# Where two of the last tiles gather their outputs: the two PSUM banks of the scores in place of two of the six common ones

## The chip, the cores and the metric

The kernel runs on one core of a Trainium2 chip. Its time is the device time of that core in microseconds (us), lower is better. The engines are TensorE (PE in the profile, with its weight loads as PEld), VectorE (DVE), ScalarE (ACT), GpSimd (POOL) and SyncE (SP), which here only issues transfers. TensorE writes its results to PSUM, a memory of eight banks; one bank holds 512 float32 values on each of 128 partitions. VectorE and ScalarE read the results from there.

## The reference, cut to what matters

An attention whose keys and values are pooled 4x4 pixels of a feature map, and behind it a gated feed-forward block:

```python
kv_pool = kv.reshape(B, H // r, r, W // r, r, C).mean(axis=(2, 4))
k = v = kv_pool.reshape(B, -1, C) @ w_sr            # 768 keys of 128 for each of 4 batches
s = (q @ k.transpose(0, 2, 1)) / sqrt(C)
a = exp(s - s.max(-1)); a /= a.sum(-1)
x = a @ v                                           # 49152 rows of 128 in all
out = (maximum(x @ w_gate, 0) * (x @ w_val)) @ w_out  # 1536 hidden units
```

The division by the row's sum is done at the end: the block is of second degree in x, so that each output row is multiplied with the squared inverse of its sum.

## The kernel before, in words

The 49152 rows are cut into 96 tiles of 512 rows (`NT = 96`, `T = 512`), numbered 0 to 95. For each tile come the scores and their exponentials (`score_block`, `exp_block`), the turned exponentials (by a DMA), the weighted values x (`values`, `keep_values`), and then the feed-forward block in twelve pieces of 128 hidden units (`NFB = 12`). For piece n of a tile:

- "v": TensorE multiplies with w_val into one bank (`value_proj`, L504); "y": ScalarE copies that to SBUF as float16 (`keep_value`, L141).
- "g": TensorE multiplies with w_gate into another bank (`gate_proj`, L515); "h": VectorE takes the maximum with 0, multiplies it with the copied value and writes the piece of hT (`gated`, L523).
- "o": TensorE multiplies the piece with w_out and adds it in the bank of the tile's output (`out_proj`; L545, or four products of 128 columns by `out_add`, L529, in the last three tiles).

The PSUM is shared out in two ways. Six banks are common: `bank()` takes the one that has stood free longest from a list, and `freed()` puts a bank back at its end when the instruction that reads it is issued. The value and gate products, x and the outputs lie there. The other two banks are one tile, `wide_ps` of 128x1024 (a pool with a single buffer), which the scores of all tiles take in turn.

The order of the work on each engine is written out by hand. `STEADY` is the list of words for one round in the middle; in a round the scores of tile k, the x of tile k-2, the v, y, g and h of tile k-3 and the o of tile k-4 are interleaved. `DRAIN` is the list for the two rounds after the last scores, `LAST` the list of the round after these. In that last round TensorE goes through o, v, g for n from 0 to 11, with o of tile 94 and v and g of tile 95.

The last three tiles, 93 to 95, take their output in the order of rows. When all twelve pieces of tile 93 have been added, the word "oT" at the end of the second `DRAIN` round makes VectorE multiply the bank with the scale (`out_scale`, L587) and SyncE store it (`out_store`, L593). Tile 94 is scaled by ScalarE (L585) after the last round. Tile 95 is done by `out_last`: 48 products in three banks, three multiplications by VectorE, and the last store from ScalarE's queue.

So around the end the order on TensorE is: ..., g of the last piece of 94, o0 of 94, v0 and g0 of 95, o1 of 94, v1 and g1 of 95, and so on. On VectorE: ..., h of the last piece of 94, the scaling of tile 93, h0 to h11 of 95, the three multiplications of the last tile.

Of the kernel before, what the change touches and what calls it, by code (L numbers as in the profile page):

```python
# [9 lines left out]
FP32 = mybir.dt.float32  # L10
# [6 lines left out]
def kernel(  # L17
# [33 lines left out]
    T = 512  # L51
    NS = T // 128
    NST = N // T
    NT = B * NST
# [67 lines left out]
    def bank(shape, dtype=FP32):  # L122
        n = asked.pop() if asked else next(n for n in free_banks if n < usable[0])
        free_banks.remove(n)
        ps = pools[n // 6].tile(shape, dtype, tag=f"bank{n}", bufs=1, name="bank_ps")
        bank_numbers[id(ps)] = n, ps
        return ps
# [3 lines left out]
    def freed(ps):  # L131
        free_banks.append(bank_numbers.pop(id(ps))[0])
        return ps
# [238 lines left out]
    hTs, o_banks, o_left, o_sbs, vals = {}, {}, {}, {}, {}  # L372
# [155 lines left out]
    def out_add(k, fb, s, o_ps, first):  # L528
        nc.tensor.matmul(  # L529
            o_ps, hTs[k][:, fb, s * 128 : (s + 1) * 128], wo16[:, fb, :],  # L530
            start=first, stop=(fb == NFB - 1), skip_group_check=True,
        )

    def out_proj(k, fb):
        if k >= NT - 3:
            if fb == 0:
                o_banks[k] = bank([128, NS, 128])
            for s in range(NS):
                out_add(k, fb, s, o_banks[k][:, s, :], fb == 0 and s == 0)
            return  # L540
        first = k not in o_banks
        if first:
            o_banks[k], o_left[k] = bank([128, T]), NFB
        o_left[k] -= 1
        nc.tensor.matmul(  # L545
            o_banks[k], wo16[:, fb, :], hTs[k][:, fb, :], start=first, stop=o_left[k] == 0
        )
# [30 lines left out]
    def out_scale(k, engine, own, o_ps=None):  # L578
        if k not in o_sbs:
            o_sbs[k] = work.tile([128, NS, 128], FP32, tag="o_sb", bufs=3, name="o_sb")  # L580
        o_sb, o_ps = o_sbs[k][:, own], o_ps if o_ps is not None else freed(o_banks[k])
        scale = squares[k // 2][:, k % 2, own]
        if engine is nc.scalar:
            for s in range(o_sb.shape[1]):
                nc.scalar.mul(o_sb[:, s], o_ps[:, s], scale[:, s : s + 1])  # L585
        else:
            nc.vector.tensor_tensor(  # L587
                o_sb, o_ps, scale.rearrange("t (s o) -> t s o", o=1).to_broadcast(list(o_sb.shape)),
                op=ALU.mult,
            )  # L590
# [11 lines left out]
    def out_last(k):  # L602
        parts = [bank([128, 2, 128]), bank([128, 1, 128]), bank([128, 1, 128])]
        owns = [slice(0, 2), slice(2, 3), slice(3, 4)]
        o_banks[k] = None

        def add(s, fb0, fb1):
            n = max(s - 1, 0)
            for fb in range(fb0, fb1):
                out_add(k, fb, s, parts[n][:, s - owns[n].start], fb == 0 and s != 1)  # L610

        def keep(n, engine, queue=nc.sync):
            out_scale(k, engine, owns[n], parts[n])
            out_store(k, owns[n], queue)

        held = NFB - 2
        add(0, 0, held)
        add(1, 0, held)
        add(2, 0, held)
        add(0, held, NFB)  # L620
        add(1, held, NFB)
        keep(0, nc.vector)
        add(2, held, NFB)
        keep(1, nc.vector)
        add(3, 0, NFB)
        keep(2, nc.vector, nc.scalar)
# [51 lines left out]
    def open_step(word):  # L678
# [90 lines left out]
        elif head == "o":  # L769
            k, n = at[0], o_left.get(at[0], NFB)  # L770
            out_proj(*at)
            for queue in (nc.gpsimd, nc.sync):
                if out_moves:
                    queue.dma_start(*out_moves.pop())
            image_step(1, k, NFB - n)
        elif head == "oT":
            out_moves.extend(out_turn(at[0]))
        elif head == "k":
            q_turn_two(2, 0)
            q_load(3, range(2))  # L780
        elif head == "s":
            if not wides:
                opening.close()
                wides.append(
                    ctx.enter_context(
                        tc.tile_pool(name="psum_wide", bufs=1, space=bass.MemoryType.PSUM)
                    )
                )
            score_block(*at)
        elif head == "e":  # L790
            k, n = at
            exp_block(k, n)
            if n % 2:
                a_turn(k, n - 1, n + 1)
        else:
            raise ValueError(word)

    out_moves, moves, spread, wides = [], [], [], []
# [21 lines left out]
    for k in range(LEAD + 2, last + 1):  # L820
# [9 lines left out]
        for word in words:  # L830
            head, n = word.rstrip("0123456789"), int(word.lstrip("abcdefghijklmnopqrstuvwxyzADPT") or 0)
            if head == "o":
                out_proj(kO, n)
                if ph == 1 and n == NFB // 2:
                    q_load(g + 2, [1])
# [7 lines left out]
            elif head == "oT":  # L843
                if kO < NT - 3:
                    out_moves.extend(out_turn(kO))
                elif k < last:
                    out_scale(kO, nc.vector, slice(0, NS))
                    out_store(kO, slice(0, NS))
# [12 lines left out]
            elif head in ("tb", "P", "pk"):  # L861
                pair, since = divmod(at - 6 if head == "tb" else at - 8, 4)
# [7 lines left out]
            elif LEAD <= kV < NT:  # L870
                if head == "x":
                    values(kV, n)
                else:
                    keep_values(kV)
    out_scale(last - LAG - 1, nc.scalar, slice(0, NS))
    out_store(last - LAG - 1, slice(0, NS))
    out_last(last - LAG)
# [30 lines left out]
```

## Time and profile before

| | us |
|---|---|
| median of 3 runs | 1024.41 (1024.4 to 1024.45) |
| the profiled execution, its own time | 1024.25 |
| its span, first to last instruction | 1022.5 |
| TensorE busy | 1017.2 (99%) |
| ScalarE busy | 918.5 (90%) |
| VectorE busy | 869.4 (85%) |
| GpSimd busy | 524.0 (51%) |

Times in the trace count from the start of the span. A row of the timeline gives the start, the length, the engine, the line, the operation with what it writes and reads, and how many equal instructions stand together. A TensorE row's length (0.38 us for a product of 512 columns) reaches over the start of the next, since products are pipelined; what TensorE needs for one is the distance from start to start. Line numbers are those of the kernel before.

### The profile page before, as it was taken

The page shows a single profiled execution, that of the slowest core. Times are in us where ns is not written, and L with a number is a line of the kernel's source. Part 1 is how long each engine was busy: PE and PEld are TensorE (multiplying, and loading weights), DVE is VectorE, ACT ScalarE, POOL GpSimd, SP SyncE. Part 2 cuts the span into 40 slices and gives each one's busy share as a digit, 9 for nine tenths or more (in the row PEclk, how much of TensorE's full clock was granted, in tenths as well). Part 3 has the DMA queues.
Part 4 walks back from the last instruction along what each step waited for, and adds up shares of the span by engine and source line. Part 5 has one row for each costly group of instructions (what it writes and reads, how often), then busy time and mean ns, then how long its engine had stood idle before and what let it go on. Part 6 is the DMA issues. An engine that isn't in the chain of part 4 may idle for free.

```text
span 1022.5 us, 17480 instructions
## 1 busy us (share of the span) xinstructions
PE 1017.2 (99%) x5021; PEld 485.2 (47%) x5021; DVE 869.4 (85%) x1450; ACT 918.5 (90%) x1927; POOL 524.0 (51%) x1312
## 2 busy tenths in 40 slices
PE   9999999999999999999999999999999999999998
PEld 4444444444444444444444444444444444444445
DVE  5988888888888888888888888888888888888888
ACT  5999998999999999999999999999999999999986
POOL 3487857344437576544434856754434543443342
PEclk9999999999999999999999999999999999999999
DMA  9999999878799999868779999978787878777651
GB/s 317 172 171 184 186 211 145 140 122 132 132 198 156 201 164 184 136 116 143 125 134 201 165 186 187 157 131 137 128 130 114 147 122 129 124 119 124 98 91 44
DMA packets 475743, 153.48 MB, mean 150 GB/s; under 512 B 451584, under 2 KB 465920, under 8 KB 475648
## 3 DMA queue, kind: packets, MB, share of 16 engines
q1 hardware_dynamic: 453184, 126.08, 65.9%
q0 software_dynamic: 22032, 25.19, 17.6%
q10 hardware_dynamic: 432, 1.11, 0.3%
q8 instruction: 39, 0.64, 0.3%
q14 instruction: 56, 0.46, 0.2%
HBM read 53.94 MB, written 26.35 MB: 79 GB/s over the span
## 4 chain that ended last, share of the span: by engine, by line
PE 99%; DMA 1%; DVE 0%; ACTq 0%; issue 0%
PE bank_ps L504 24%; PE bank_ps L515 24%; PE bank_ps L545 24%; PE wide_ps L397 12%; PE bank_ps L439 12%; PE bank_ps L529 1%; DMA kv_in<-in_kv_dram 1%; PE bank_ps L456 1%; PE bank_ps L378 1%; PE wide_ps L336 0%; PE bank_ps L300 0%; PE bank_ps L314 0%; PE bank_ps L474 0%; DVE kv_s L272 0%; PE bank_ps L209 0%; ACTq L246 0%
## 5 line engine op out<-in xcount | busy, mean ns | idle before, releaser
L523 DVE SCALAR_TENSOR_TENSOR hT<-bank_ps,val 128x512 f16<-128x512 f32 x1152 | 727.3, 679 | 104.4 <-PE bank_ps L515 83.7
L141 ACT CAST val<-bank_ps 128x512 f16<-128x512 f32 x1149 | 628.4, 596 | 44.4 <-PE bank_ps L504 23.9
L504 PE MATMUL bank_ps<-xT,wv 128*128 128x512 f16 x1152 | 421.0, 379 | 0.0
L515 PE MATMUL bank_ps<-xT,wg 128*128 128x512 f16 x1152 | 376.3, 379 | 0.0
L545 PE MATMUL bank_ps<-hT,wo 128*128 128x512 f16 x1116 | 348.7, 379 | 0.0
L402 ACT ACTIVATE a<-wide_ps 128x768 f16<-128x768 f32 x368 | 302.2, 821 | 44.0 <-PE wide_ps L397 44.0
L397 PE MATMUL wide_ps<-kv,qT 128*128 128x512 f16 x736 | 179.8, 326 | 0.0
L439 PE MATMUL bank_ps<-aT,kv 128*128 128x512 f16 x552 | 179.0, 379 | 0.0
L558 POOL TENSOR_TENSOR o_sb<-o_t,scale 128x512 f32<-128x512 f32 x89 | 93.2, 1047 | 158.8 <-issue 141.0
L545 PEld LDWEIGHTS <-wo 128*128 128x128 f16 x1116 | 109.1, 98 | 132.1 <-issue 0.5
L515 PEld LDWEIGHTS <-wg 128*128 128x128 f16 x1152 | 112.6, 98 | 122.5 <-issue 0.2
L504 PEld LDWEIGHTS <-wv 128*128 128x128 f16 x1152 | 112.5, 98 | 105.4 <-issue 0.4
L423 POOL COPY scale<-square 32x8 f32<-32x8 f32 x736 | 141.2, 192 | 28.6
L416 POOL TENSOR_TENSOR square<-inverse 128x8 f32<-128x8 f32 x46 | 9.3, 202 | 248.9 <-DVE inverse L414 248.9
L838 POOL DMA_DIRECT2D out_dram<-o_sb x208 | 130.3, 632 | 9.6 <-POOL o_sb L558 7.4
L397 PEld LDWEIGHTS <-qT 128*128 128x128 f16 x736 | 71.9, 98 | 87.0 <-issue 0.2
L447 DVE CAST xT<-bank_ps 128x512 f16<-128x512 f32 x92 | 63.6, 691 | 31.7 <-PE bank_ps L439 31.6
L439 PEld LDWEIGHTS <-kv 128*128 128x128 f16 x552 | 53.9, 98 | 65.2
L402 ACT ACTIVATION_READ_ACCUMULATOR a<-wide_ps 128x1 f32 x368 | 76.1, 207 | 0.0
L553 DVE STREAM_TRANSPOSE o_t<-bank_ps 128x512 f32<-128x512 f32 x93 | 65.4, 703 | 0.3 <-PE bank_ps L504 0.2
L162 POOL DMA_DIRECT2D q<-in_q_dram x84 | 48.8, 581 | 0.3 <-issue 0.3
L256 POOL TENSOR_TENSOR s<-kv_in 128x512 f32<-128x512 f32 x36 | 45.1, 1281 | 0.7
(86 smaller groups left out, 210.8 us busy)
## 6 DMA issues: line engine op xcount, KB each, us to landing
kv_in<-in_kv_dram SPq DMA_DIRECT2D x42, 512.0 KB, 5.3
out_dram<-o_sb SPq DMA_DIRECT2D x177, 64.0 KB, 3.6
q<-in_q_dram POOLq DMA_DIRECT2D x88, 128.0 KB, 3.4
out_dram<-o_sb POOLq DMA_DIRECT2D x176, 64.0 KB, 4.2
aT<-a SPq DMA_TRANSPOSE x184, 4.5
kv_line<-in_kv_dram SPq DMA_DIRECT2D x4, 512.0 KB, 9.8
placed<-blocks SPq DMA_DIRECT2D x9, 128.0 KB, 2.5
kvT<-placed SPq DMA_DIRECT2D x36, 32.0 KB, 2.2
```

What stands on the lines that cost most here:

```text
L141: nc.scalar.copy(to, what)
L397: nc.tensor.matmul(s_ps[:, j0 * 128 : j1 * 128], qT, kv16[:, b, j0:j1, 0:C], start=True, stop=True)
L402: nc.scalar.activation(a16s[k][:, s, :], s_banks.pop(s)[:, 0:J], AF.Exp, scale=qk_scale, accum_out=a_sums[k // 2][:, k % 2, s : s + 1],)
L423: nc.gpsimd.tensor_copy(to[32 * b : 32 * (b + 1), :, :, j], squares[k // 2][32 * j : 32 * (j + 1)])
L439: nc.tensor.matmul(x_banks[k], kv16[:, k // NST, jc, C : 2 * C], aT[:, jc], start=first, stop=x_left[k] == 0,)
L504: nc.tensor.matmul(proj_banks["v", k, fb], wv16[:, fb * 128 : (fb + 1) * 128], xTs[k], start=True, stop=True,)
L515: nc.tensor.matmul(proj_banks["g", k, fb], wg16[:, fb * 128 : (fb + 1) * 128], xTs[k], start=True, stop=True,)
L523: nc.vector.scalar_tensor_tensor(hTs[k][:, fb, :], freed(proj_banks.pop(("g", k, fb))), 0.0, vals.pop((k, fb)), op0=ALU.max, op1=ALU.mult,)
L545: nc.tensor.matmul(o_banks[k], wo16[:, fb, :], hTs[k][:, fb, :], start=first, stop=o_left[k] == 0)
L553: nc.vector.transpose(o_t, freed(o_banks.pop(k)))
L558: nc.gpsimd.tensor_tensor(to, o_by, scale.to_broadcast([128, NS, 4, 32]), op=ALU.mult)
L838: queue.dma_start(*out_moves.pop())
```

## The change

The gathering bank of tiles 93 and 94 is no longer taken by `bank()` at each tile's first piece. At the first piece of tile 93 one `wide_ps` tile is taken from the pool of the scores, and its two halves of 512 columns, a bank each, become the gathering places of tiles 93 and 94. The scores of all tiles are done by then. `out_scale` no longer gives a bank back, since none was taken from the list. Nothing else is edited; the lists of words and the number of instructions stay as they are.

```diff
     def out_proj(k, fb):
         if k >= NT - 3:
-            if fb == 0:
-                o_banks[k] = bank([128, NS, 128])
+            if k == NT - 3 and fb == 0:
+                pair = wides[0].tile([128, 1024], FP32, tag="wide", name="wide_ps")
+                for i in range(2):
+                    o_banks[k + i] = pair[:, i * T : (i + 1) * T].rearrange(
+                        "t (s c) -> t s c", s=NS
+                    )
             for s in range(NS):
                 out_add(k, fb, s, o_banks[k][:, s, :], fb == 0 and s == 0)
             return
@@
-        o_sb, o_ps = o_sbs[k][:, own], o_ps if o_ps is not None else freed(o_banks[k])
+        o_sb, o_ps = o_sbs[k][:, own], o_ps if o_ps is not None else o_banks[k]
```

## The prediction

> **What bounds the kernel now.** I read the page's engine shares and its chain first, then the stretches around the change, then the timelines of the three engines there. The page says that the chain which ended last is TensorE almost alone.
>
> ```profile
> PE 1017.2 (99%) x5021; PEld 485.2 (47%) x5021; DVE 869.4 (85%) x1450; ACT 918.5 (90%) x1927; POOL 524.0 (51%) x1312
> ...
> PE 99%; DMA 1%; DVE 0%; ACTq 0%; issue 0%
> ```
>
> The change touches nothing ahead of the first output product of tile 93, the first of these in TensorE's timeline, so only the last 20 us are in question.
>
> ```profile
> 1002.14 0.61 PE L529 MATMUL bank_ps<-wo,hT 128*128 128x128 f16 x8
> ```
>
> The stretches there (PE, PEld, DVE, ACT and POOL busy, then the granted clock):
>
> ```profile
> 1000.00:1005.00 5.00, 5.00 (x43) 2.99 (x42) 4.97 (x9) 3.99 (x9) 3.70 (x6) 1.00 0.16 26
> 1005.00:1010.00 5.00, 5.00 (x52) 3.26 (x49) 4.74 (x9) 3.06 (x6) 1.74 (x4) 1.00 0.19 30
> 1010.00:1015.00 5.00, 5.00 (x45) 3.14 (x45) 5.00 (x8) 4.25 (x8) 0.00 (x0) 1.00 0.14 52
> ```
>
> TensorE and VectorE are both full here, and the granted clock is 1.00. Whether TensorE waits at all is seen from start to start:
>
> ```profile
> 1008.06 0.38 PE L515 MATMUL bank_ps<-xT,wg 128*128 128x512 f16 x1
> 1008.27 0.39 PE L529 MATMUL bank_ps<-wo,hT 128*128 128x128 f16 x4
> 1008.50 0.38 PE L504 MATMUL bank_ps<-xT,wv 128*128 128x512 f16 x1
> 1008.71 0.38 PE L515 MATMUL bank_ps<-xT,wg 128*128 128x512 f16 x1
> 1008.93 0.39 PE L529 MATMUL bank_ps<-wo,hT 128*128 128x128 f16 x4
> 1009.15 0.38 PE L504 MATMUL bank_ps<-xT,wv 128*128 128x512 f16 x1
> 1009.45 0.38 PE L515 MATMUL bank_ps<-xT,wg 128*128 128x512 f16 x1
> 1009.66 0.39 PE L529 MATMUL bank_ps<-wo,hT 128*128 128x128 f16 x4
> 1010.05 0.39 PE L504 MATMUL bank_ps<-xT,wv 128*128 128x512 f16 x1
> 1010.27 0.38 PE L515 MATMUL bank_ps<-xT,wg 128*128 128x512 f16 x1
> ...
> 1015.95 0.38 PE L504 MATMUL bank_ps<-xT,wv 128*128 128x512 f16 x1
> 1016.17 0.38 PE L515 MATMUL bank_ps<-xT,wg 128*128 128x512 f16 x1
> 1016.42 2.84 PE L529 MATMUL bank_ps<-wo,hT 128*128 128x128 f16 x48
> ```
>
> 1008.06 is the gate product of tile 94's last piece, 1008.27 is o0 of tile 94, 1008.50 and 1008.71 are v0 and g0 of tile 95, and so on; 1010.05 is v2, 1016.17 is g11, and the 48 products are the last tile's. Unhindered, a product starts 0.21 to 0.23 after the one before, and a group of o, v, g takes 0.66 (1008.93 - 1008.27). Between 1008.27 and 1010.05 lie seven steps, three o at 0.225 and four v or g at 0.215, which is 1.535; 1.78 passed. So TensorE loses 0.25 here to waits for banks (0.09 at g1, 0.17 at v2), and after v2 almost nothing: (1016.17 - 1010.27) / 9 = 0.656 a group. All that this stage could give back is that 0.25, and some 0.03 ahead of the 48 products. VectorE and ScalarE:
>
> ```profile
> 1005.48 3.92 DVE L523 SCALAR_TENSOR_TENSOR hT<-bank_ps,val 128x512 f16<-128x512 f32 x6 [0.19 <-ACT val L141]
> 1009.31 0.68 DVE L587 TENSOR_TENSOR o_sb<-bank_ps,square 128x512 f32<-128x512 f32 x1
> 1009.91 7.77 DVE L523 SCALAR_TENSOR_TENSOR hT<-bank_ps,val 128x512 f16<-128x512 f32 x12
> ```
> ```profile
> 1008.91 1.24 ACT L141 CAST val<-bank_ps 128x512 f16<-128x512 f32 x2 [1.12 <-PE bank_ps L504]
> 1010.48 6.48 ACT L141 CAST val<-bank_ps 128x512 f16<-128x512 f32 x10 [0.32 <-PE bank_ps L504]
> ```
> ```profile
> PEld L504 <- DVE o_sb L587: 0.2, 1, 0.2
> ```
>
> VectorE runs six h pieces of tile 94 without a gap, 0.65 each, and scales tile 93 right behind them: that ends at 1009.31 + 0.68 = 1009.99, 1.72 after o0 of tile 94 was begun. v2 at 1010.05 is the product that got tile 93's bank: it started 0.06 after the scaling ended, which the wait above names.
>
> **The change part by part.** *The first half.* o0 of tile 93 used to wait for a copy by ScalarE that freed its bank; now it takes the scores' banks, whose last reader finished over a round ago. Cost nothing, gain nothing: that product started without a gap before.
>
> *One more common bank.* While tile 93 gathers, and again while tile 94 does, v and g turn over six banks, not five. The most this can give is the 0.28 above, least nothing; the next part takes it all.
>
> *The second half, and a new wait.* Tiles 93 and 94 now share one tile, `wide_ps`. The tile framework keeps order tile by tile, and in the program as built o0 of tile 94, the first product into the second half, waits for VectorE's scaling of tile 93, the last reader of the first half. Before, o0 had a bank of its own and waited only for an h piece four instructions earlier on VectorE. No row shows the new wait itself; its ends are known. TensorE reaches o0 at 1008.27; the scaling ends at 1009.99. I take 0.06 for the hand-over, as at v2, so that o0 starts at 1010.05: a stall of 1.78. It cannot be shorter by much, since VectorE has no gap from 1005.48 on and its inputs came from a TensorE that was not held up until then; the 0.19 gap before, which waited for a ScalarE copy, is the most that could come off it. The ends are thus 1.59 and, with the 0.2 of the waits row as the hand-over, 1.92.
>
> *What is queued behind it.* Products start in order, so v0, g0 and all that follows of tile 95 come later, as do ScalarE's copies and VectorE's h0 to h11. After o0 come the same steps: v2 starts at 1010.05 + 1.535 = 1011.585, not at 1010.05, which is +1.535; the 0.25 of waits before is in that difference, since it falls away.
>
> *Whether the rest catches up or falls further behind.* TensorE can't catch up: from v2 on it goes at 0.656 a group before and after, and before only the 0.03 at 1016.42 can be won. Does VectorE hold it up? A copy starts 0.41 after its v (1008.91 - 1008.50) and, from the last, ends 1.01 after it (1010.48 + 6.48 - 1015.95); h11 ends 1.73 after v11 (1009.91 + 7.77 - 1015.95). With six banks v of piece n+3 takes the bank of v of piece n: free after 1.01, wanted after 1.97. g of piece n+3 takes that of g: free after 1.73, wanted after 2.19. That leaves 0.4 after the hand-over, and h at 0.65 keeps pace with groups of 0.656. VectorE's head start is gone (its queue idles from 1009.99 until h0 at about 1011.4), but nothing waits for it. In the last tile, the first product that needs h10 comes after g11's step of 0.22 and 30 of the 48 products, 30 x 2.84 / 48 = 1.78: 2.2 after v11, while even h11 is ready after 1.73. So the 48 products start about 1.5 later and run as before, and the last multiplications and stores follow them as before. Tile 93's store is issued at the same time as before, since its scaling is; ScalarE's scaling of tile 94 and its store move with tile 94, and end ahead of the last tile's as they did. No instruction or transfer is added on any queue.
>
> The sum: +1.535 less 0.03, say **+1.5 us**. Against the profiled execution's 1024.25 that is 1025.75; its 1024.25 lies 0.16 under the median of the runs, 1024.41, so that I put the changed kernel at **1025.9**, 0.15% slower. A difference of under 0.2% (2.05 us, up to 1026.46) is counted as no change here.
>
> **A rule beside the row.** The Trainium skill's page "PSUM — Partial Sum Buffer", section "PSUM bank collisions raise a hardware error", says that accesses are to be guarded by bank and quadrant. The two halves are different banks, so by that rule the chip asks for no wait here, and o0 would start at 1008.27; the sum would be the gain of at most 0.28, or 1024.1. No run here shows two engines in the two halves at once, and the wait that the program holds decides, so the sum goes by that.
>
> **The rivals.**
> *No wait between the halves.* The two halves hold different data, and nothing in the computation orders them. Then only the sixth bank counts: 1024.41 - 0.28 to 1024.41, say 1024.2. Against it stands the wait in the built program.
> *Slower than 0.2%: the granted clock falls in the pause.* TensorE's longest pause in these 20 us is now 0.17; the new one is ten times that. If the clock were halved after it, a group would take 1.31 in place of 0.66. From 0.55 us of loss on (1026.46 - 1025.9), so 1.1 us at half clock, the change counts as slower. Ends: no time at half clock, 1025.9; all that is left, twelve groups of 0.656 and 2.84, which is 10.7 us more. If it lasts as long as the pause, it is 0.9 more: 1026.8. No row of before has a granted clock under 1.00, so nothing in it speaks for this. The Trainium skill, "TensorE: Matmul & The Clock Gate", part 1, gives the half clock to an idle window of about 3.4 us; by that rule a pause of 1.78 is too short, and the time stays 1025.9.
> *VectorE becomes the bound of the last round.* It now starts h0 without a backlog and has 0.4 of slack per piece; a hand-over 0.05 slower on each of twelve pieces would eat it and add 0.2 to 0.6: 1026.1 to 1026.5. Against it: the 12 pieces of before already run at 0.65 each.
>
> **How the numbers follow.** The new wait with its price of 1.5: 0.74. VectorE as the bound: 0.09, a third of it beyond 1026.46. The clock: 0.12, nearly all beyond. No wait between the halves: 0.03. Something that I don't see: 0.02, on either side. So slower by over 0.2%: 0.16; within 0.2%: 0.83; faster: 0.01, since 0.28 is all there is to win. The range goes from 1025.3 (the stall shortened by 0.19, a profile that stands 0.16 closer to the runs and some 0.2 for the readings) to 1026.7 (a hand-over of 0.2, VectorE's 0.6).
>
> **What would show it.** In TensorE's timeline a gap of about 1.8 ahead of the first four L529 products of tile 94, at 1008.3 to 1010.05, put down to VectorE's scaling; VectorE idle for some 1.4 after it and h pieces that then follow v by 1.7; no gap at g1 and v2; the 48 products at about 1017.95; a span of about 1024.0; the granted clock at 1.00. I am wrong if o0 starts at 1008.3 (no wait), if the groups after it take over 0.66 (the clock or VectorE), or if the scaling itself comes at another time.

## The result, and the profile after

The changed kernel takes 1025.84 us in the median of 22 runs (1025.63 to 1026.69), the kernel before 1024.40 in 22 (1024.2 to 1024.82). The ratio is 1.0015, with a 95% interval of 1.0009 to 1.0021: 1.44 us slower, where 1.5 was forecast.

The profiled execution of the changed kernel took 1026.69, 0.85 over its median. The waits of TensorE over its whole span say where that came from. A row names who waited, for whom, and for how long in total, how often, and the longest:

```profile
PE wide_ps L529 <- DVE o_sb L591: 1.6, 1, 1.6
...
PE bank_ps L439 <- DMA aT<-a: 0.8, 1, 0.8
```

The second row is a late transfer of turned exponentials, work that the change doesn't touch; TensorE has no such wait in the profile of before. It leaves everything behind it 0.95 us later than before (the gate product of tile 94's last piece starts at 1009.01, there at 1008.06), so places are compared from that product on. The first row is the new wait. TensorE's timeline around it (line 529 keeps its number, 587 has become 591):

```profile
1009.01 0.38 PE L515 MATMUL bank_ps<-xT,wg 128*128 128x512 f16 x1
1011.00 0.38 PE L529 MATMUL wide_ps<-wo,hT 128*128 128x128 f16 x4 [1.61 <-DVE o_sb L591]
1011.22 0.38 PE L504 MATMUL bank_ps<-xT,wv 128*128 128x512 f16 x1
1011.43 0.38 PE L515 MATMUL bank_ps<-xT,wg 128*128 128x512 f16 x1
1011.65 0.39 PE L529 MATMUL wide_ps<-wo,hT 128*128 128x128 f16 x4
1011.87 0.38 PE L504 MATMUL bank_ps<-xT,wv 128*128 128x512 f16 x1
1012.09 0.38 PE L515 MATMUL bank_ps<-xT,wg 128*128 128x512 f16 x1
1012.31 0.39 PE L529 MATMUL wide_ps<-wo,hT 128*128 128x128 f16 x4
1012.53 0.38 PE L504 MATMUL bank_ps<-xT,wv 128*128 128x512 f16 x1
1012.75 0.38 PE L515 MATMUL bank_ps<-xT,wg 128*128 128x512 f16 x1
...
1018.64 0.38 PE L515 MATMUL bank_ps<-xT,wg 128*128 128x512 f16 x1
1018.86 2.84 PE L529 MATMUL bank_ps<-wo,hT 128*128 128x128 f16 x48
```

o0 of tile 94 starts 1.99 after the gate product, not 0.21: a stall of 1.78 from start to start. The trace counts 1.61, since it lets the gate product's 0.38 run out first; below, "pause" is this shorter figure. From o0 to the 48 products there is no other gap. VectorE and ScalarE in the same stretch:

```profile
1006.43 3.92 DVE L523 SCALAR_TENSOR_TENSOR hT<-bank_ps,val 128x512 f16<-128x512 f32 x6 [0.19 <-ACT val L141]
1010.26 0.68 DVE L591 TENSOR_TENSOR o_sb<-wide_ps,square 128x512 f32<-128x512 f32 x1
1012.25 7.90 DVE L523 SCALAR_TENSOR_TENSOR hT<-bank_ps,val 128x512 f16<-128x512 f32 x12 [1.31 <-PE bank_ps L504]
```
```profile
1011.63 7.79 ACT L141 CAST val<-bank_ps 128x512 f16<-128x512 f32 x12 [2.89 <-PE bank_ps L504]
```

The scaling of tile 93 ends at 1010.94, and o0 follows 0.06 later. VectorE, which went on to h0 at once before, now idles 1.31 for it.

### The profile page after: what moved, and what is told of

It reads as the page before. It is cut to its first block, busy times and chain, and to the rows that moved or that the text cites. A ratio compares the mean times of both kernels' runs of the same rounds, so it can differ in the third digit from the quotient of the medians.

```text
span 1024.9 us, 17486 instructions
## 1 busy us (share of the span) xinstructions
PE 1017.0 (99%) x5021; PEld 485.4 (47%) x5021; DVE 869.9 (85%) x1450; ACT 919.5 (90%) x1927; POOL 524.7 (51%) x1312
## 4 chain that ended last, share of the span: by engine, by line
PE 97%; DMA 2%; DVE 0%; issue 0%; ACTq 0%; DVEq 0%
PE bank_ps L504 24%; PE bank_ps L515 24%; PE bank_ps L549 23%; PE wide_ps L397 12%; PE bank_ps L439 12%; DMA aT<-a 1%; DMA kv_in<-in_kv_dram 1%; PE bank_ps L456 1%; PE bank_ps L378 1%; PE wide_ps L529 0%; PE wide_ps L336 0%; PE bank_ps L300 0%; PE bank_ps L529 0%; PE bank_ps L314 0%; DVE hT L523 0%; PE bank_ps L474 0%
```

## The experiments

All times are medians; those of before are from runs on the same chip, beside each. The runs with three and with one and a half scalings were on another chip than the others. The theory is that the loss is one wait, of the first product into the second half for the reader of the first half, and that it is there only because both halves have one name. The rival is that the place costs: these banks, or the clock.

**The same banks under two names.** The pool of `wide_ps` is closed ahead of tile 93 and a pool of two one-bank tiles opened in its place.

```diff
-                pair = wides[0].tile([128, 1024], FP32, tag="wide", name="wide_ps")
+                scores_psum.close()
+                tail = ctx.enter_context(tc.tile_pool(name="psum_tail", bufs=1, space=PSUM))
                 for i in range(2):
-                    o_banks[k + i] = pair[:, i * T : (i + 1) * T].rearrange(...)
+                    o_banks[k + i] = tail.tile([128, NS, 128], FP32, tag=f"tail{i}", name="tail_ps")
```

> The changed kernel, but the two banks of the scores are handed over as two tiles of one bank each, one for tile 93 and one for tile 94; the banks, the order of the work and the instructions stay. Theory (the wait is one between the two halves, there only because they have one name): o0 of tile 94 no longer waits for VectorE's scaling of tile 93, the stall of 1.78 us is gone, and the sixth common bank gives back up to 0.28: 1024.1 to 1024.4. Rival (the place costs, whatever it is called: these banks, or the clock after them): 1025.8 as in the changed kernel.

Measured: 1024.03 (1023.83 to 1024.39, 11 runs), beside 1024.37 for before; ratio 0.9997 (0.9988 to 1.0006). The timeline of TensorE, from the same gate product:

```profile
1008.48 0.38 PE L516 MATMUL bank_ps<-xT,wg 128*128 128x512 f16 x1
1008.70 0.39 PE L530 MATMUL tail_ps<-wo,hT 128*128 128x128 f16 x4
...
1010.01 0.39 PE L530 MATMUL tail_ps<-wo,hT 128*128 128x128 f16 x4
...
1016.34 0.38 PE L516 MATMUL bank_ps<-xT,wg 128*128 128x512 f16 x1
1016.56 2.84 PE L530 MATMUL bank_ps<-wo,hT 128*128 128x128 f16 x48
```
```profile
1009.73 0.68 DVE L593 TENSOR_TENSOR o_sb<-tail_ps,square 128x512 f32<-128x512 f32 x1
```

o0 starts 0.22 after the gate product, and from the gate product to the 48 products pass 8.08 us, in the kernel before 8.36: the pause is gone, and so are the 0.28 of waits for want of a sixth bank. While VectorE scales tile 93 out of one of the two banks (1009.73 to 1010.41), TensorE adds o2 of tile 94 in the other, from 1010.01 on. The stall came from the shared name, not from the place. That this version is faster than the kernel before is seen in the trace; the medians say the same, but the ratio's interval doesn't leave 1.

**Half of the change: only tile 93 in the scores' banks.**

```diff
-                for i in range(2):
-                    o_banks[k + i] = pair[:, i * T : (i + 1) * T].rearrange(...)
+                o_banks[k] = pair[:, 0:T].rearrange("t (s c) -> t s c", s=NS)
+            elif fb == 0:
+                o_banks[k] = bank([128, NS, 128])
```

> Half of the change: tile 93 gathers in the scores' banks, tile 94 in a common bank. Theory: no stall at o0 of tile 94; five banks for v and g in the last round as before, so v3 waits about 0.2 us for h0: 1024.3 to 1024.4. Rival (the place costs): half of the loss at least, 1025.1 or more.

Measured: 1024.31 beside 1024.37, ratio 1.0002 (0.9994 to 1.0011). No stall at o0; v3 is the late product, with 0.41 from the start before it where 0.22 is the rule. VectorE begins h0 at 1010.01 and needs some 0.69 for it, which agrees with the forecast that v3 waits for it:

```profile
1010.34 0.39 PE L529 MATMUL bank_ps<-wo,hT 128*128 128x128 f16 x4
1010.75 0.38 PE L504 MATMUL bank_ps<-xT,wv 128*128 128x512 f16 x1
```

**The other half: only tile 94 there**, in the second bank, with tile 93's common bank given back after its scaling.

```diff
-            if k == NT - 3 and fb == 0:
+            if k == NT - 2 and fb == 0:
                 pair = wides[0].tile([128, 1024], FP32, tag="wide", name="wide_ps")
-                for i in range(2):
-                    o_banks[k + i] = pair[:, i * T : (i + 1) * T].rearrange(...)
+                o_banks[k] = pair[:, T : 2 * T].rearrange("t (s c) -> t s c", s=NS)
+            elif fb == 0:
+                o_banks[k] = bank([128, NS, 128])
...
-                    out_scale(kO, nc.vector, slice(0, NS))
+                    out_scale(kO, nc.vector, slice(0, NS), freed(o_banks[kO]))
```

> The other half: tile 93 gathers in a common bank, which comes back after its scaling, tile 94 in the second bank of the scores. Theory: no reader of the first half, so no stall at o0; g2 is the product that gets tile 93's bank, wanted at about the time when the scaling ends: 1024.1 to 1024.4. Rival (the place costs): 1025.1 or more.

Measured: 1024.14 beside 1024.37, ratio 0.9999 (0.999 to 1.0008). o0 starts 0.21 after the gate product. Either half alone costs nothing that can be measured; only the two together do.

**The wait kept, but covered.** The o of tile 94 stands three pieces later in the last round.

```diff
-    LAST = [f"{head}{n}" for n in range(NFB) for head in "ovygh"] + ["oT"]
+    LAST = [
+        word for n in range(NFB + 3)
+        for word in [f"o{n - 3}"] * (n >= 3) + [f"{head}{n}" for head in "vygh"] * (n < NFB)
+    ] + ["oT"]
```

> The changed kernel, with the o of tile 94 put three pieces later in the last round's list: v0, g0, v1, g1, v2, g2 of tile 95 come first, then o0. Theory: the wait stays, but 1.29 us of products cover it; 0.49 of it is left, and g3 waits some 0.16 for h0: 0.65 in place of 1.78, about 1024.7, between 1024.4 and 1025.0. Rival (the place or the clock costs): 1025.8.

Measured: 1024.82 beside 1024.37, ratio 1.0006 (0.9997 to 1.0015).

```profile
1009.18 0.38 PE L507 MATMUL bank_ps<-xT,wv 128*128 128x512 f16 x1
1009.49 0.38 PE L518 MATMUL bank_ps<-xT,wg 128*128 128x512 f16 x1
1010.09 0.38 PE L532 MATMUL wide_ps<-wo,hT 128*128 128x128 f16 x4 [0.22 <-DVE o_sb L594]
1010.31 0.38 PE L507 MATMUL bank_ps<-xT,wv 128*128 128x512 f16 x1
1010.69 0.38 PE L518 MATMUL bank_ps<-xT,wg 128*128 128x512 f16 x1
```

Against steps of 0.215, g2 is 0.09 late, o0 0.38 and g3 0.16: 0.63 in all, where 0.65 was expected (0.49 at o0, of which g2 has already taken 0.09, and 0.16 at g3). The same wait for the same scaling costs a third as much when TensorE has other products to run first.

**The reader on another engine.** ScalarE scales tile 93.

```diff
-                    out_scale(kO, nc.vector, slice(0, NS))
+                    out_scale(kO, nc.scalar, slice(0, NS))
```

> The changed kernel, with tile 93 scaled by ScalarE, which idles there, in place of VectorE: four instructions of 1.14 us together, free to start at about 1008.3 by the times of before, when the last o product of tile 93 is in its bank, not behind two h pieces. Theory: o0 of tile 94 starts at about 1009.5 in place of 1010.05, the stall is some 1.2: about 1025.3. Rival (the stall has to do with VectorE's read of a PSUM bank or with the clock, not with the last reader of the first half): no stall, 1024.1 to 1024.4, or 1025.8.

Measured: 1025.26 beside 1024.40, ratio 1.0009 (1.0 to 1.0018). The pause follows the reader, whichever engine it is on:

```profile
1008.24 0.38 PE L515 MATMUL bank_ps<-xT,wg 128*128 128x512 f16 x1
1009.68 0.38 PE L529 MATMUL wide_ps<-wo,hT 128*128 128x128 f16 x4 [1.06 <-ACT o_sb L589]
```
```profile
1008.49 1.14 ACT L589 ACTIVATE o_sb<-wide_ps,square 128x128 f32<-128x128 f32 x4 [0.52 <-PE wide_ps L529]
```

ScalarE ends at 1009.63 and o0 starts 0.05 later; the stall is 1009.68 - 1008.24 - 0.21 = 1.23.

**The wait made longer.** The scaling issued twice.

```diff
                     out_scale(kO, nc.vector, slice(0, NS))
+                    out_scale(kO, nc.vector, slice(0, NS))
```

> The changed kernel, with VectorE's scaling of tile 93 issued twice, one right behind the other (the second writes the same values again). Theory: o0 of tile 94 waits for the second, which ends 0.60 to 0.68 later (1009.31 to 1009.91 is start to start, 0.68 one length): the stall grows to about 2.4 and the time to 1026.4 to 1026.5. Rival (the stall is of a fixed length, or VectorE's queue has room): 1025.8.

Measured: 1027.03, seven runs from 1026.39 to 1028.21, beside 1024.40; ratio 1.0029 (1.0018 to 1.004). The profiled execution, 1026.56, shows a longer pause and nothing else. From start to start the stall is 2.50, where about 2.4 was expected; the pause is 2.33, 0.72 over the changed kernel's 1.61:

```profile
PE wide_ps L529 <- DVE o_sb L591: 2.3, 1, 2.3
```

But the median is above the forecast of 1026.4 to 1026.5, and the runs lie in two groups. So it was run again, and beside it the two tiles of the first experiment with the scaling issued twice.

> The shared tile with two scalings once more, since its seven runs lay between 1026.39 and 1028.21. Theory: the stall is 0.65 to 0.72 longer than with one scaling, as its trace shows, and what goes beyond 1026.5 is scatter that comes from elsewhere: a median of 1026.4 to 1026.6. Rival: a median of 1027 again, so that the second scaling costs about twice its length.

> The two banks handed over as two tiles, and tile 93 scaled twice by VectorE. Theory: o0 of tile 94 still doesn't wait; the second scaling moves h0 0.65 later, and g3, which gets g0's bank when h0 has read it and was ready 0.09 before that with one scaling, now waits some 0.6: about 1024.6, 0.6 over the two tiles with one scaling and 1.8 or more under the shared tile with two. Rival (two scalings cost by themselves more than their 0.65, as the median of the shared tile with two, 1.2 over that with one, may say): 1025.2 or more.

Measured: 1028.20 for the shared tile (seven runs, 1026.56 to 1028.42), ratio 1.0031 (1.002 to 1.0042): the forecast of 1026.4 to 1026.6 failed. The two tiles with two scalings took 1024.75 (1024.59 to 1024.82, 11 runs) beside 1024.32, ratio 1.0004 (0.9995 to 1.0013), where about 1024.6 was forecast; there, a second scaling costs about its length (0.72) and no more. The second profile of the shared tile is of an execution of 1028.42, and shows the rest. Stretches (busy times of PE, PEld, DVE, ACT and POOL, then the granted clock):

```profile
1005.00:1010.00 5.00, 3.73 (x42) 2.51 (x39) 4.76 (x8) 2.34 (x5) 2.02 (x4) 1.00 0.21 34
1010.00:1012.00 2.00, 0.94 (x9) 0.64 (x9) 0.98 (x2) 0.30 (x1) 0.00 (x0) 0.91 0.06 22
1012.00:1014.00 2.00, 2.00 (x12) 1.17 (x11) 1.21 (x2) 0.87 (x2) 0.00 (x0) 0.50 0.29 110
1014.00:1016.00 2.00, 2.00 (x14) 1.15 (x13) 0.92 (x3) 1.18 (x3) 0.00 (x0) 0.73 0.00 0
1016.00:1018.00 2.00, 2.00 (x20) 1.29 (x19) 2.00 (x4) 1.79 (x4) 0.00 (x0) 1.00 0.00 0
```

and its products:

```profile
1011.07 0.38 PE L529 MATMUL wide_ps<-wo,hT 128*128 128x128 f16 x4 [2.33 <-DVE o_sb L591]
1011.29 0.38 PE L504 MATMUL bank_ps<-xT,wv 128*128 128x512 f16 x1
1011.50 0.48 PE L515 MATMUL bank_ps<-xT,wg 128*128 128x512 f16 x1
1011.77 0.63 PE L529 MATMUL wide_ps<-wo,hT 128*128 128x128 f16 x4
...
1013.05 0.63 PE L529 MATMUL wide_ps<-wo,hT 128*128 128x128 f16 x4
...
1014.76 0.53 PE L504 MATMUL bank_ps<-xT,wv 128*128 128x512 f16 x1
1015.13 0.38 PE L515 MATMUL bank_ps<-xT,wg 128*128 128x512 f16 x1
```

About 0.6 us after the pause has ended, the granted clock falls to 0.50; a group of o, v, g takes 1.28 (1013.05 - 1011.77) in place of 0.656, until about 1015. Each execution comes with its mean granted clock: in the two sets, seven had a mean clock of 1.000 and a median of 1026.59, seven had 0.998 and a median of 1028.20. The fall costs 1.6 us. This was the rival of the halved clock, which the changed kernel's own pause did not bring about. The next two runs move the pause.

```diff
                     out_scale(kO, nc.vector, slice(0, NS))
+                    out_scale(kO, nc.vector, slice(0, NS))
+                    out_scale(kO, nc.vector, slice(0, NS))
```

> The shared tile with three scalings of tile 93, so that TensorE pauses for about 3.05 us (2.33 with two). With two, the profile of one execution shows the granted clock at 0.50 behind the pause and that of another at 1.00, and seven of fourteen executions took about 1.7 us more. Theory (a pause beyond some length lets the clock fall, the sooner the longer it is): nearly all executions show it, so 1027.1 (1026.5 and one more scaling of 0.65) and 1.7, about 1028.8; those without it about 1027.1. Rival (the fall has nothing to do with the pause): again half of them, or none.

```diff
                     out_scale(kO, nc.vector, slice(0, NS))
+                    again = slice(NS // 2, NS)
+                    out_scale(kO, nc.vector, again, o_banks[kO][:, again])
```

> The shared tile, with half of tile 93's columns scaled a second time: 256 columns took 0.425, so that the pause is about 2.0 us, between the 1.61 of the changed kernel, where none of 22 executions shows a halved clock, and 2.33. Theory (the same): 1026.2, with some executions, fewer than half, 1.7 higher; none of them if the limit lies above 2.0. Rival (the fall has nothing to do with the pause): half of them.

Measured: three scalings 1028.71 (five runs, 1027.44 to 1028.94), ratio 1.0038 (1.0026 to 1.0051); one and a half 1028.02 (seven runs, 1026.24 to 1028.13), ratio 1.0031 (1.002 to 1.0042), both beside 1024.47. About 1028.8 was forecast for the first, which held. For the second it was 1026.2 with fewer than half of the executions higher, and that failed. A TensorE wait of each, three scalings first:

```profile
PE wide_ps L529 <- DVE o_sb L591: 3.1, 1, 3.1
```
```profile
PE wide_ps L529 <- DVE o_sb L591: 2.1, 1, 2.1
```

| pause of TensorE, us | kernel | executions with a mean clock under 0.9995 and a time 1.2 or more over the group's lowest |
|---|---|---|
| 0.53 | two tiles, scaled twice | 0 of 11 |
| 1.06 | scaled by ScalarE | 0 of 11 |
| 1.61 | the changed kernel | 0 of 22 |
| 2.07 | scaled one and a half times | 6 of 7 |
| 2.33 | scaled twice, both sets | 7 of 14 |
| 3.06 | scaled three times | 4 of 5 |

A pause does bring the fall: it came in 17 of 26 executions with a pause of 2.07 or more, and in none of 44 with a shorter one. (One execution of the changed kernel, 1026.28, has a mean clock of 0.999 and no trace. Such a mean alone says little: in the profile of the covered wait it comes from a fall at 1021.75, behind TensorE's last product, which costs no time.) But that it comes the more often the longer the pause, as was expected, is not shown: 2.07 had it more often than 2.33.

The traces show more of what decides. In each of the twelve profiles the record of the clock at 1.00 begins 4.3 to 6.9 us after the start, and from there to the first fall it lasts a whole number of periods of 3.413 us (295, 298 or 299 of them). Each of the three half-clock stretches ahead of the last product lasts one such period too. So the clock changes at the ends of periods, and where these lie differs from execution to execution. Two profiles have the same pause of 2.33, and only the second a fall. Their periods, with TensorE's busy time as the first number behind the length, and the granted clock third from the end:

```profile
1006.92:1010.33 3.41, 1.62 (x18) 0.99 (x16) 3.33 (x6) 0.98 (x2) 0.00 (x0) 1.00 0.07 12
1010.33:1013.74 3.41, 2.86 (x29) 1.92 (x29) 2.10 (x4) 2.02 (x4) 0.00 (x0) 1.00 0.21 77
```
```profile
1008.24:1011.65 3.41, 1.08 (x12) 0.63 (x10) 2.70 (x5) 0.00 (x0) 0.00 (x0) 1.00 0.00 0
1011.65:1015.06 3.41, 3.41 (x19) 2.04 (x17) 1.68 (x3) 1.75 (x3) 0.00 (x0) 0.50 0.20 77
```

In the first, a period's end cuts the pause into 1.79 and 0.55; in the second, all 2.33 lie in one period, and the clock is halved for the next. Over all whole periods of the twelve records, the time after the last product included, every one with 2.07 us or more without a product ended in a fall (14 of them), and none with 1.87 or less did. The changed kernel's 1.61 lay whole in one period (1008.53 to 1011.94), and brought none. This is read out of the traces; no run moves the pause against the periods, and for the executions without a trace it isn't shown.

## Why the prediction was right

**The new wait.** Forecast: o0 of tile 94 waits for the scaling of tile 93, a stall of 1.78, hand-over 0.06. Measured: 1.78 and 0.06. The scaling begins 1.25 after the gate product in both kernels (1009.31 - 1008.06, 1010.26 - 1009.01), since VectorE is full up to it and its inputs come from a TensorE that has not yet waited. That is what made the price readable before any run.

**The old waits swallowed by it.** Forecast: v2 would be 1.535 late, not 1.78, because 0.25 of waits for banks falls away. From o0 to v2 pass 1.53 (1011.00 to 1012.53) and none of the seven steps is late. Without the new wait, the two tiles win these 0.28 back (8.08 in place of 8.36).

**No catching up and no falling back.** From g2 to g11 a group takes (1018.64 - 1012.75) / 9 = 0.654, before 0.656. The 48 products start 9.85 after the gate product, before 8.36: +1.49, forecast +1.5. A copy begins 0.41 after its v (1011.63 - 1011.22), as reckoned; VectorE idles 1.31, forecast some 1.4. The rival that VectorE would become the bound did not come.

**No wait between the halves.** The rule of the Trainium skill's page "PSUM — Partial Sum Buffer" (section "PSUM bank collisions raise a hardware error"), that accesses are guarded by bank, describes what the two tiles do: TensorE writes one bank while VectorE reads the other (1010.01 in the trace of that run), at 1024.03. For the chip the wait was not needed; for the shared tile the program held it, and that decided, as the prediction put it.

**The clock.** The rival was right in kind and mis-sized. It took the half clock to last as long as the pause, and so to cost 0.9 us; the runs show one period of 3.413 us whatever the pause, and 1.6 us a time. It was held against it that a pause of 1.78 is too short by the Trainium skill ("TensorE: Matmul & The Clock Gate", part 1: an idle window of about 3.4 us). For the changed kernel that held: none of its 22 executions shows such a fall. But the reason was too strong. The traces agree with the length of the page's window, 3.413 us, but not with its being idle throughout: between 1.87 and 2.07 us of idleness in one are enough. A pause of 2.07 brought the fall in 6 of 7 executions. So the changed kernel stayed under the limit by 0.26 to 0.46 us, which the prediction couldn't know, and in that it was lucky; half a scaling more made that rival the usual case, at 1028.0, beyond the range.

**The total.** 1025.84 against 1025.9, inside 1025.3 to 1026.7, as are all 22 runs (the highest is 1026.69, the execution with the late transfer).

## What to carry to other kernels

Two results that only share an allocation also share its waits: if the second is begun while the first is still being read, give each bank a name of its own, or put other work between. When a bank is gained and a wait is added, price the wait at the place where it falls, from the end of the work it waits for, less what it swallows; here each half of the change was free, and the two together cost 1.44 us. And keep pauses of a full TensorE short: here, from about 2 us on, the pause was often not all that was paid.

## What was not expected of the hardware

After a pause of TensorE of 2.07 us or more, the granted clock fell in 17 of 26 executions, which cost 1.6 us; after 1.61 us it did so in none of 22. Three of the 17 have a trace, and in each the clock was 0.50 for one period of 3.413 us; the others are told by their mean clock and their time. In all twelve traces the falls stand at the ends of such periods, and only where one held 2.07 us or more without a product. So the fall can come when TensorE is already at work again: with a pause of 2.33 the first two steps still ran at full speed, with one of 3.06 only the first.
